# Attention masked by hashes with a maxout feed-forward layer: shorter zero products, a reshuffled first head, later bursts, halves of added weights added, own buffers for the last rows

## The chip, the core and the metric

The kernel runs on one core of one Trainium2 chip. A core has five engines that run at the same time, each with its own stream of instructions that it works through in order: TensorE (PE in the profile, with its weight loads as PEld), VectorE (DVE), ScalarE (ACT), GpSimd (POOL) and SyncE (SP), which here only issues DMAs. Engines wait for each other by semaphores. The metric is the device time of one execution in microseconds (us). The kernel before takes 277.81 us (median of 3 runs, 276.68 to 278.61).

## What is computed

The input is `q`, `k` and `v` for 4 batches of 8 heads with 768 positions of 64 numbers, a projection `proj` of 64 by 6, and the weights of a feed-forward layer (three matrices of 512 by 768 and `w_out` of 768 by 512). The core of the reference:

```
q_bits = (einsum('bhsd,dk->bhsk', q, proj) > 0)      # 6 sign bits per position
k_bits = (einsum('bhsd,dk->bhsk', k, proj) > 0)
mask   = bucket(q_bits)[..., :, None] == bucket(k_bits)[..., None, :]
scores = where(mask, q @ k^T / 8, -1e9)
attn   = softmax(scores)                             # over the keys
x      = (attn @ v), heads side by side              # 3072 rows of 512
h      = max(x @ w1, x @ w2, x @ w3)
out    = h @ w_out
```

The output is 3072 rows of 512 numbers in fp32.

## The kernel before, in words

**How the mask is made.** For each head the kernel keeps a tile `S` that holds, in bf16, the transposed and scaled 64 rows of q and k and below them rows with the sign bits as +0.5 and -0.5. One product of such columns gives the score plus a term that is largest where all bits agree; with the bias of the exponential, other keys fall to almost nothing.

**Chunks and units.** Queries are worked on in chunks: batch 0 has three chunks of 256 queries (chunks 0 to 2), batches 1 to 3 have two chunks of 384 each (chunks 3 to 8). A *unit* (`scores`, L277) is one chunk, one head and a part of the keys. For chunks 3 to 8 it is two score products of 384 columns (L293) and one exponential on ACT over 128 x 768 elements (L301), which writes a tile `AT` of unnormalized weights in fp16. There are 192 units; units 0 to 47 belong to batch 0, and each later chunk has 24. The 24 `AT` tiles are used in turn.

**Adding weights.** The softmax needs the sum of a query's weights over all keys. For chunks 3 to 8 the three `AT` tiles of a head (six blocks of 128 keys, two to a tile) are first added on DVE (`add`, L317 to L324): two additions of 128 x 768 per head, which leave a tile `ad` with two blocks of 384 columns. The additions of a unit are recorded two units later.

**Bursts.** When four heads of a chunk (a half chunk, 12 units in chunks 3 to 8) are through, `burst` (L333) runs three pieces: `sums` (L345) multiplies the blocks of `ad` by ones, 8 products for chunks 3 to 8, then a short chain on DVE turns the result into reciprocals (L352 to L356: transposition, addition, reciprocal, transposition back); `values`, twice, multiplies the weights by v (L367, 24 products each), and DVE scales the result into `xT` (L374). `LAG` sets how many units after its last unit a burst stands: 1 for chunks 0 to 2 (whose bursts have partly fixed places), 2 for the later ones (L557).

**Feed-forward.** A chunk's feed-forward layer is a list of groups (`ffn_groups`, L385): 18 groups of four products (L396), each followed by a copy (ACT, L401; DVE, L403, for chunks 0 to 2) or a maximum on DVE (L405), and then for each 128 rows two half groups of three products with `w_out` (L433), a copy to `osb` on ACT (L437) and a DMA to the output on SP's queue (L439). The pool of `osb` has two buffers. About one group (1.15 per unit after batch 0) is placed after the scores of a unit. The last 128 rows of the last chunk are made in two halves (`last`, L410): one is copied by ACT (L418) and sent from ACT's queue, the other by DVE (L420) and sent from SP's queue; each half takes an `osb` tile of its own.

**Banks.** The sums, values, hashes and feed-forward groups write to four PSUM banks handed out in turn (`bank`, `give`); scores have their own two. A product that gets a bank must wait until the engine that read its former content is through.

**Loads and transpositions.** Heads 0 to 7 of batch 0 are transposed on PE (`pair_turn`, L120), copied to fp32 tiles `T32` (`pair_keep`), hashed (`head_hash` L167 with `head_bits` L172, or `pair_hash`) and placed into `S` (`pair_place` on POOL, L134, or `first_place` on ACT, L161). For later batches, sets of four heads are transposed on DVE (`turn`, L198: eight transpositions of 128 x 384 for the q and k of a set), narrowed on POOL (L203), placed by DMAs on SP's queue (L208), and hashed by 16 products (`quad_hash`, L217) whose bits are made on DVE (L220) and placed by DMAs on SP's queue (L228). `hash_at` gives the unit of that hash: 11 units before the set is needed. v and the feed-forward weights are loaded by DMAs that POOL issues (L236, L244).

**Order.** The whole order is written out by hand inside `manual_schedule`: the loop at L572 records, unit by unit, the next scores, then the work due at this unit, then feed-forward groups, then bursts. Each engine works in this order; only the semaphores' waits decide the time. Before the loop stands the opening (L449 to L507): loads, clearing of tiles, 12 products of zeros (L472), and the first head's path to the first unit.

Of the kernel before, what the change touches and what calls it, by code (L numbers as in the profile page):

```python
# [9 lines left out]
FP32 = mybir.dt.float32  # L10
# [7 lines left out]
def kernel(  # L18
# [34 lines left out]
    NAT = 24  # L53
    LAG = 1
    ATW = 776
# [23 lines left out]
    at_tiles = [konst.tile([P, ATW], FP16, name=f"AT{i}", tag=f"AT{i}") for i in range(NAT)]  # L79
    warm = at_tiles[-1][:, 0:HALF]  # L80
    w_sb = [konst.tile([P, NJC, DF], FP16, name=f"w{i}_sb", tag=f"w{i}_sb") for i in range(3)]
# [6 lines left out]
    def bank():  # L88
        i = free_banks.pop(0)
        return i, bank_tiles[i]  # L90

    def give(i):
        free_banks.append(i)
# [69 lines left out]

    def head_hash(bp, pi, side, hd):
        for par in range(2):
            j = 2 * side + par
            nc.tensor.matmul(bp[Q * j : Q * j + NBITS, 0:HALF], pj2[:, par : 2 * NBITS : 2],  # L167
                             t32[pi][:, side, hd * HALF : (hd + 1) * HALF], start=True, stop=True)
# [105 lines left out]
    def block_of(b, m):  # L274
        return 2 * (m % MH) + m // MH if b == 0 else m
# [41 lines left out]
    def add(c, h, n):  # L317
        w = chunks[c][2]
        t = [blocks(at_tiles[at_of[unit_at[c, h, i]]], w)[:, :, 0:w] for i in range(n + 1)]
        if n == 1:  # L320
            sum_of[c, h] = ad_pool.tile([P, 2, HALF], FP16, tag="ad", name="ad")
        else:
            t[0] = sum_of[c, h][:]
        nc.vector.tensor_tensor(out=sum_of[c, h][:], in0=t[0], in1=t[n], op=AluOp.add)  # L324

    def sum_blocks(c, h):
        w = chunks[c][2]
        if (c, h) in sum_of:
            t = sum_of[c, h]
            return [t[:, j, 0:w] for j in range(2)]  # L330
        return [weights_of(c, h, m)[:, 0:w] for m in range(NM)]
# [53 lines left out]
    def ffn_groups(c):  # L385
# [22 lines left out]
        rows = out[b * S : (b + 1) * S, :].rearrange("(p c) m -> c p m", c=NM)  # L408

        def last(part, tb):  # L410
            k_, ps = bank()
            cs = slice(part * DM // 2, (part + 1) * DM // 2)
            for fb in range(NFB):
                nc.tensor.matmul(ps[:, 0 : DM // 2], hts[fb][:, tb * P : (tb + 1) * P], wout_sb[:, fb, cs],
                                 start=(fb == 0), stop=(fb == NFB - 1))
            osb = o_pool.tile([P, DM], FP32, tag="osb", name="osb")
            if part == 0:
# [6 lines left out]
        for tb in range(w // P):  # L424
            def go2(part, tb=tb):
# [9 lines left out]
                if part == 1:  # L435
                    osb = o_pool.tile([P, DM], FP32, tag="osb", name="osb")
                    nc.scalar.copy(osb[:], ps[:, 0:DM])  # L437
                    give(k_)
                    nc.sync.dma_start(rows[block_of(b, q0 // P + tb)], osb[:])  # L439
            gs += [lambda go2=go2: go2(0), lambda go2=go2: go2(1)]  # L440
# [7 lines left out]
    with tc.manual_schedule():  # L448
# [9 lines left out]
        load_pair(3, nc.sync)  # L458
        nc.gpsimd.memset(pj[:], 0.0)
        nc.vector.memset(pj2[:], 0.0)  # L460
# [3 lines left out]
        for hd in range(2):  # L464
            for u in range(2):
                nc.vector.tensor_copy(pj2[hd * D + u * Q : hd * D + (u + 1) * Q, hd : hd + 2 * NBITS - 1 : 2], pst[:, u, :])
        for x in range(4):
            nc.gpsimd.tensor_copy(pj[x * Q : (x + 1) * Q, :, x : x + 4 * NBITS - 3 : 4], pst[:])
        load_v(0)
        iw, wp = bank()  # L470
        for n in range(12):
            nc.tensor.matmul(wp[:, 0:HALF], warm[:, 0:P], warm, start=True, stop=True)  # L472
        give(iw)
# [3 lines left out]
        ib, bk = bank()  # L477
        i1, mk1 = bank()
        bq = sc_ps.tile([P, 2, 512], FP32, tag="sc", name="bp")[:, 0, :]
        pair_turn(0, 1, 0, mk)  # L480
        pair_turn(0, 0, 0, mq)
        pair_keep(0, 1, 0, mk)
        pair_keep(0, 0, 0, mq)
        head_hash(bk, 0, 1, 0)
        head_hash(bq, 0, 0, 0)
        pair_turn(0, 1, 1, mk1)
        first_place(1, 0, 0, mk)
        head_bits(bk, 0, 1, 0, 0)
        first_place(0, 0, 0, mq)
        head_bits(bq, 0, 0, 0, 0)  # L490
        give(iq)
        first_place(1, 0, 1, mk)
        head_bits(bk, 0, 1, 0, 1)
        give(ik)
        give(ib)
        pair_place(0, 0, 1, 0, 1)
        i2, mq1 = bank()
        pair_turn(0, 0, 1, mq1)
        pair_keep(0, 1, 1, mk1, nc.scalar)
        give(i1)  # L500
        scores(0)
        head_bits(bq, 0, 0, 0, 1)
        pair_keep(0, 0, 1, mq1, nc.scalar)
        give(i2)
        for side in (1, 0):
            for par in range(2):
                pair_place(0, side, par, 1, 2)  # L507

        for pi, us in ((1, ((0, 1, 0), (0, 0, 0), (3, 1, 1), (4, 0, 1))), (2, ((6, 1, 0), (7, 1, 1), (8, 0, 0), (9, 0, 1))),
# [26 lines left out]
        for g in range(2, NQUAD):  # L536
            b2, i2 = divmod(g, 2)
            need = UPB * b2 + 12 * i2
            for n, side in enumerate((1, 0)):
# [9 lines left out]
                when(t0 + 6, place, name, range(4))  # L549
            hash_at[{2: 33, 3: 47}.get(g, need - 11)] = g  # L550
            when({2: 36, 3: 46}.get(g, need - 22), load_v, g)
# [4 lines left out]
        for c, i in sorted(done_at, key=lambda e: done_at[e]):  # L556
            d = done_at[c, i] + (LAG if c < 3 else 2)  # L557
            sums, values = burst(c, i)
# [67 lines left out]
```

## Time and profile before

One execution was profiled. Its own time was 277.43 us, of which the span from its first to its last instruction is 275.6 us.

| | |
|---|---|
| median of 3 runs | 277.81 us |
| profiled execution: time, span | 277.43 us, 275.6 us |
| PE busy | 263.2 us (95%) |
| DVE busy | 196.0 us (71%) |
| ACT busy | 179.1 us (65%) |
| POOL busy | 68.0 us (25%) |
| sum products (L345) | 240 |
| additions of weights (L324) | 96, mean 551 to 572 ns |
| mean granted TensorE clock | 0.992 |

Busy time is time in which an engine executes; a matmul's end is modelled, so that the row of a product shows some 0.16 us more than the distance to the next one. The *view of waits* lists who waited for whom; the *chain* follows the work that ended last back from the end; the *table by stretches* gives busy times, the granted TensorE clock and DMA load between two times; the *timeline* lists instructions with the idle time of their engine before them and what ended it, in brackets.

### The profile page before, as it was taken

Reading aid. Unit: us, or ns where it says so; the run is one execution under the profiler, and the core shown is the slowest. Engines: PE = TensorE matmul, PEld = TensorE weight load, DVE = VectorE, ACT = ScalarE, POOL = GpSimd, SP = SyncE. Lnnn points to the kernel's source line nnn. Section 1 sums busy time; section 2 is a strip of 40 time slices with the busy share of each in tenths; the row PEclk is TensorE's granted clock in tenths of the full one; section 3 lists DMA queues with packets and bytes.
Section 4 is the critical chain, followed back from the end, with each engine's and each line's share of the span. In section 5 each row is a group of like instructions: output and inputs, shape, how many; then the busy total and the mean of one; then the engine's idle time right before and its main releaser. Section 6 shows DMA issues by size and latency. Waiting matters only on the chain.

```text
span 275.6 us, 6502 instructions
## 1 busy us (share of the span) xinstructions
PE 263.2 (95%) x2538; PEld 158.6 (58%) x2538; DVE 196.0 (71%) x486; ACT 179.1 (65%) x260; POOL 68.0 (25%) x108
## 2 busy tenths in 40 slices
PE   7899999999999979999999999999999999999992
PEld 3555667865666645565555555555555555555651
DVE  3686787965886996996684898797657674865440
ACT  2888876648767860966859586683868769571321
POOL 3699550374100350285000062140000000000000
PEclk9999999999999997999999999999999999999999
DMA  7979999979921157169912036622020003001203
GB/s 226 287 158 165 221 245 227 209 125 231 246 49 40 38 145 115 53 183 251 168 40 76 2 81 148 160 57 63 33 95 0 1 4 114 2 0 40 76 2 114
DMA packets 20398, 30.97 MB, mean 112 GB/s; under 512 B 2608, under 2 KB 14736, under 8 KB 20368
## 3 DMA queue, kind: packets, MB, share of 16 engines
q0 software_dynamic: 8384, 14.16, 26.9%
q1 hardware_dynamic: 11552, 15.88, 19.2%
q10 hardware_dynamic: 432, 0.52, 0.6%
q8 instruction: 20, 0.33, 0.5%
q14 instruction: 10, 0.08, 0.1%
HBM read 25.17 MB, written 6.29 MB: 114 GB/s over the span
## 4 chain that ended last, share of the span: by engine, by line
PE 86%; DVE 7%; ACT 2%; issue 2%; DMA 1%; DVEq 0%; ACTq 0%
PE ms L396 31%; PE sc L293 22%; PE ms L367 11%; PE ms L433 11%; PE ms L345 4%; PE ms L217 3%; ACT AT L301 2%; DVE ad L324 2%; PE ms L472 1%; DVE ht L405 1%; PE ms L120 1%; PE ms L147 1%; PE ms L167 1%; DVE S L172 1%; DMA out_dram<-osb 1%
## 5 line engine op out<-in xcount | busy, mean ns | idle before, releaser
L301 ACT ACTIVATE AT<-sc 128x768 f16<-128x768 f32 x192 | 152.7, 816 | 66.4 <-PE sc L293 58.6
L396 PE MATMUL ms<-xT,w_sb 128*128 128x384 f16 (+1 forms) x648 | 115.0, 308 | 0.7 <-DVE ht L405 0.7
L293 PE MATMUL sc<-S 72*128 72x384 bf16 (+1 forms) x432 | 93.5, 308 | 2.6 <-ACT AT L301 1.9
L396 PEld LDWEIGHTS <-w_sb 128*128 128x128 f16 x648 | 62.6, 97 | 36.9 <-issue 1.5
L405 DVE TENSOR_TENSOR ht<-ht,ms 128x384 f16<-128x384 f16 (+1 forms) x108 | 54.3, 503 | 37.3 <-PE ms L396 35.4
L293 PEld LDWEIGHTS <-S 72*128 72x128 bf16 (+1 forms) x432 | 39.5, 98 | 34.0 <-issue 14.1
L203 POOL TENSOR_SCALAR T<-T 128x768 bf16<-128x768 f32 x24 | 21.8, 907 | 101.2 <-DVE T L198 80.4
L367 PE MATMUL ms<-AT,vo 128*32 128x385 f16 (+3 forms) x864 | 37.7, 318 | 0.0
L433 PE MATMUL ms<-wout_sb,ht 128*128 128x512 f16 x138 | 35.4, 378 | 0.0
L367 PEld LDWEIGHTS <-vo 128*32 128x32 f16 x864 | 25.1, 99 | 9.3 <-issue 1.3
L324 DVE TENSOR_TENSOR ad<-AT,AT 128x768 f16<-128x768 f16 x48 | 27.4, 572 | 2.8 <-ACT AT L301 2.8
L324 DVE TENSOR_TENSOR ad<-ad,AT 128x768 f16<-128x768 f16 x48 | 26.5, 551 | 2.5 <-ACT AT L301 1.2
L198 DVE STREAM_TRANSPOSE T<-nat 128x384 f32<-128x384 f32 x48 | 26.6, 561 | 0.0
L401 ACT CAST ht<-ms 128x384 f16<-128x384 f32 x36 | 17.2, 477 | 8.8 <-PE ms L396 8.7
L374 DVE SCALAR_TENSOR_TENSOR xT<-ms,sv,rb 128x384 f16<-128x384 f32 (+1 forms) x36 | 19.9, 568 | 2.6 <-PE ms L367 1.3
L433 PEld LDWEIGHTS <-ht 128*128 128x128 f16 x138 | 13.3, 97 | 13.3 <-DVE ht L405 0.8
L437 ACT COPY osb<-ms 128x512 f32<-128x512 f32 x23 | 13.4, 582 | 10.7 <-PE ms L433 9.6
L352 DVE STREAM_TRANSPOSE ys<-ms 128x384 f32<-128x384 f32 (+1 forms) x18 | 9.7, 536 | 8.0 <-PE ms L345 7.8
L134 POOL TENSOR_SCALAR S<-T 64x384 bf16<-64x384 f32 (+1 forms) x21 | 13.2, 627 | 3.8 <-ACT T L127 1.6
L192 POOL DMA_DIRECT2D nat<-in_k_dram x20 | 11.1, 563 | 3.6 <-DMA nat<-in_k_dram 2.2
L192 POOL DMA_DIRECT2D nat<-in_q_dram x20 | 11.1, 566 | 2.7 <-DMA vo<-in_v_dram 1.8
L345 PEld LDWEIGHTS <-ones 128*32 128x32 f16 x240 | 5.4, 95 | 8.8 <-issue 8.7
(48 smaller groups left out, 121.9 us busy)
## 6 DMA issues: line engine op xcount, KB each, us to landing
out_dram<-osb SPq DMA_DIRECT2D x23, 256.0 KB
S<-T SPq DMA_DIRECT2D x48, 96.0 KB
nat<-in_k_dram POOLq DMA_DIRECT2D x20, 192.0 KB, 7.5
nat<-in_q_dram POOLq DMA_DIRECT2D x20, 192.0 KB, 7.1
vo<-in_v_dram POOLq DMA_DIRECT2D x8, 384.0 KB, 8.2
w_sb<-in_moe_w_dram POOLq DMA_DIRECT2D x3, 768.0 KB, 7.2
nat<-in_k_dram SPq DMA_DIRECT2D x6, 192.0 KB
nat<-in_k_dram SPq DMA_DIRECT2D x3, 384.0 KB
```

Of the source, the lines that this page charges most:

```text
L192: eng.dma_start(dst, src)
L198: nc.vector.transpose(t32[name][:, u, half * HALF : (half + 1) * HALF], i_)
L203: nc.gpsimd.tensor_scalar(out=t16[name][:, u, :], in0=t32[name][:, u, :], scalar1=RS, scalar2=1.0, op0=AluOp.mult, op1=AluOp.mult)
L293: nc.tensor.matmul(views[j], s_of[kn][0 : D + bits, kx, m * P : (m + 1) * P], s_of[qn][0 : D + bits, qx, q0 : q0 + w], start=True, stop=True)
L301: nc.scalar.activation(t[:, :, 0:w], whole, ActFn.Exp, bias=-SCALE * 0.25 * bits, scale=SCALE)
L324: nc.vector.tensor_tensor(out=sum_of[c, h][:], in0=t[0], in1=t[n], op=AluOp.add)
L367: nc.tensor.matmul(av[Q * x : Q * (x + 1), 0:n], v_at[2 * b + i][:, x, cb * D + side : (cb + 1) * D : 2], weights_of(c, 4 * i + x, m)[:, 0 ...
L374: nc.vector.scalar_tensor_tensor(out=xt_of(c)[:, 2 * i + side, 0:w], in0=av[:, 0:w], scalar=sv_of[b, i, side][:], in1=rb[0][:, 0:w], op0=A ...
L396: nc.tensor.matmul(ps[:, 0:w], w_sb[wi][:, jc, fb * P : (fb + 1) * P], xt[:, jc, 0:w], start=(jc == 0), stop=(jc == NJC - 1))
L401: nc.scalar.copy(hts[fb][:, 0:w], ps[:, 0:w])
L405: nc.vector.tensor_tensor(out=hts[fb][:, 0:w], in0=hts[fb][:, 0:w], in1=ps[:, 0:w], op=AluOp.max)
L433: nc.tensor.matmul(ps[:, 0:DM], hts[fb][:, tb * P : (tb + 1) * P], wout_sb[:, fb, :], start=(fb == 0), stop=(fb == NFB - 1))
```

## The change

- `warm`, the tile for the zero products, is 256 columns at another place of the last `AT` tile; 14 products of 256 columns replace 12 of 384. It is cleared in one instruction as before, of 256 instead of 384 columns.
- Opening: two of the four copies into the projection `pj2` go from DVE to POOL. Clearing and filling `pj` and the first load of v go from POOL's beginning to the end of the opening. The first head's k is kept by DVE and its q by ACT (both by DVE before); its placing is three times POOL and once ACT (before: three times ACT, once POOL); the hash products of k and q alternate; the first unit's scores stand before the second head's transpositions; the second head is kept by DVE instead of ACT.
- `LAG` becomes `(1, 4)`: bursts of chunks 3 to 8 stand four units behind instead of two.
- For chunks 4 to 8, after a head's second addition, DVE adds the second block of `ad` to the first (128 x 384), and `sums` reads one block: 4 products instead of 8.
- The last chunk's rows go to slices of one tile from the pool of loads, one slice per 128 rows, instead of the two `osb` buffers.
- The hash of a set stands 9 units ahead instead of 11.

```diff
-    LAG = 1
+    LAG = (1, 4)
-    warm = at_tiles[-1][:, 0:HALF]
+    warm = at_tiles[-1][:, THIRD + 2 : 2 * THIRD + 2]
...
         nc.vector.tensor_tensor(out=sum_of[c, h][:], in0=t[0], in1=t[n], op=AluOp.add)
+        if n == 2 and c > 3:
+            t = sum_of[c, h]
+            nc.vector.tensor_tensor(out=t[:, 0, :], in0=t[:, 0, :], in1=t[:, 1, :], op=AluOp.add)
...
-            return [t[:, j, 0:w] for j in range(2)]
+            return [t[:, j, 0:w] for j in range(1 if c > 3 else 2)]
...
+        def out_rows(tb):
+            if c < NCH - 1:
+                return o_pool.tile([P, DM], FP32, tag="osb", name="osb")
+            if "end" not in nat:
+                nat["end"] = nat_pool.tile([P, 4 * NM * D], FP32, tag="nat", name="nat")
+            return nat["end"][:, tb * DM : (tb + 1) * DM]
...
-        nc.gpsimd.memset(pj[:], 0.0)
...
             for u in range(2):
-                nc.vector.tensor_copy(pj2[hd * D + u * Q : hd * D + (u + 1) * Q, hd : hd + 2 * NBITS - 1 : 2], pst[:, u, :])
-        for x in range(4):
-            nc.gpsimd.tensor_copy(pj[x * Q : (x + 1) * Q, :, x : x + 4 * NBITS - 3 : 4], pst[:])
-        load_v(0)
+                (nc.vector, nc.gpsimd)[hd].tensor_copy(
+                    pj2[hd * D + u * Q : hd * D + (u + 1) * Q, hd : hd + 2 * NBITS - 1 : 2], pst[:, u, :])
         iw, wp = bank()
-        for n in range(12):
-            nc.tensor.matmul(wp[:, 0:HALF], warm[:, 0:P], warm, start=True, stop=True)
+        for n in range(14):
+            nc.tensor.matmul(wp[:, 0:THIRD], warm[:, 0:P], warm, start=True, stop=True)
...
         pair_keep(0, 1, 0, mk)
-        pair_keep(0, 0, 0, mq)
-        head_hash(bk, 0, 1, 0)
-        head_hash(bq, 0, 0, 0)
-        pair_turn(0, 1, 1, mk1)
-        first_place(1, 0, 0, mk)
+        pair_keep(0, 0, 0, mq, nc.scalar)
+        give(ik)
+        for par in range(2):
+            pair_place(0, 1, par, 0, 1)
+        first_place(0, 0, 0, mq)
+        give(iq)
+        pair_place(0, 0, 1, 0, 1)
+        for par in range(2):
+            head_hash(bk, 0, 1, 0, (par,))
+            head_hash(bq, 0, 0, 0, (par,))
         head_bits(bk, 0, 1, 0, 0)
-        first_place(0, 0, 0, mq)
         head_bits(bq, 0, 0, 0, 0)
+        scores(0)
+        i1, mk1 = bank()
+        pair_turn(0, 1, 1, mk1)
...
+        nc.gpsimd.memset(pj[:], 0.0)
+        for x in range(4):
+            nc.gpsimd.tensor_copy(pj[x * Q : (x + 1) * Q, :, x : x + 4 * NBITS - 3 : 4], pst[:])
+        load_v(0)
...
-            hash_at[{2: 33, 3: 47}.get(g, need - 11)] = g
+            hash_at[{2: 33, 3: 47}.get(g, need - 9)] = g
...
-            d = done_at[c, i] + (LAG if c < 3 else 2)
+            d = done_at[c, i] + LAG[c > 2]
```

## The prediction

> **What bounds the kernel now.** First the page's busy times: PE works 95% of the span, so a microsecond saved elsewhere counts only where PE stands still, at half clock, or has work removed.
>
> ```profile
> span 275.6 us, 6502 instructions
> PE 263.2 (95%) x2538; PEld 158.6 (58%) x2538; DVE 196.0 (71%) x486; ACT 179.1 (65%) x260; POOL 68.0 (25%) x108
> PEclk9999999999999997999999999999999999999999
> ```
>
> One slice of the clock is not full. The view of waits, for PE alone, shows where it stands:
>
> ```profile
> PE sc L293 <- ACT AT L301: 1.9, 4, 0.6
> PE ms L345 <- DVE ad L324: 1.8, 2, 1.4
> PE ms L472 <- DVE AT L463: 1.7, 1, 1.7
> ```
>
> Then the table by stretches (columns: length, then PE, PEld, DVE, ACT, POOL busy with instructions, clock, DMA share, GB/s). The first three rows lie between the sum products of one half chunk and the next: (3,0) to (3,1), on to (4,0), on to (4,1). The next two are the same for chunk 6, the last two are shorter.
>
> ```profile
> 74.11:87.85 13.74, 13.11 (x131) 8.38 (x130) 11.09 (x37) 9.58 (x14) 0.00 (x0) 1.00 0.26 64
> 87.85:103.96 16.11, 13.54 (x139) 9.16 (x139) 14.77 (x37) 10.51 (x14) 6.20 (x8) 1.00 0.33 96
> 103.96:121.44 17.48, 17.48 (x146) 10.31 (x145) 14.56 (x31) 10.64 (x16) 5.23 (x7) 0.90 0.46 105
> 154.27:169.17 14.90, 14.90 (x129) 8.29 (x128) 14.30 (x32) 10.71 (x16) 6.12 (x8) 1.00 0.28 76
> 169.17:186.31 17.14, 17.14 (x153) 9.88 (x152) 14.53 (x31) 11.79 (x19) 3.98 (x5) 1.00 0.50 115
> ...
> 100.62:104.03 3.41, 1.54 (x17) 0.92 (x18) 3.31 (x9) 1.00 (x2) 1.85 (x2) 1.00 0.30 69
> 104.04:107.46 3.42, 3.42 (x48) 2.09 (x51) 2.38 (x6) 0.00 (x0) 0.00 (x0) 0.50 1.05 143
> ```
>
> In the half chunks in which DVE also transposes a set, it is nearly full. In 87.85 to 103.96 it is the bound; the timeline shows the sum products waiting for its additions:
>
> ```profile
> 103.36 0.55 DVE L324 TENSOR_TENSOR ad<-ad,AT 128x768 f16<-128x768 f16 x1
> 103.83 0.41 DVE L403 CAST ht<-ms 128x256 f16<-128x256 f32 x1
> 103.96 0.75 PE L345 MATMUL ms<-ad,ones 128*32 128x384 f16 x5 [1.45 <-DVE ad L324]
> ```
>
> After 3.41 us with PE busy for 1.54, the clock is 0.50 for 3.42 us: 1.7 us lost.
>
> **Opening: taken as 0.** The zero products start at 1.67, behind DVE's clearing of the last weights tile, and the changed program still waits for that clearing. They stand 0.32 us apart; twelve would end at 5.51, yet the first transposition starts at 5.27, so the rate doubles near 5.05. Fourteen of 256 columns at 2/3 of 0.32 end at 1.67 + 3.0 = 4.6: transpositions start 0.67 earlier, the first 1.6 at half rate (0.27), the rest at 0.137 (six in 0.82). But the first bits decide:
>
> ```profile
> 6.87 0.82 PE L167 MATMUL bp<-T,pj 128*6 128x384 f32 x4
> 7.27 0.56 DVE L172 TENSOR_SCALAR S<-ms 6x384 bf16<-6x384 f32 x1 [0.46 <-PE ms L167]
> 8.46 0.49 PE L293 MATMUL sc<-S 70*128 70x256 bf16 x3
> ```
>
> In the changed program the first bits wait for the third hash product (k, second half), behind one of q that needs ACT's copy of q. They end at 4.6 + 0.45 + 0.6 = 5.65, ACT's copy (0.48) ends at 6.30, the third product starts at 6.63, bits at 7.26: as before. Bounds: 0.9 earlier if the third product isn't waited for, 0.6 later if the transpositions stay slow. The six transpositions now between units 0 and 1 (0.82) fill the 0.69 us in which PE waited there. POOL gets two placings more (0.5 each) and, behind the second head's placing, the clearing, four copies and load of v that stood ahead (1.1 + 0.94), so that its queue to 33 us runs 3 us late: loads of k, w1, q and w2 are behind it. Its placings for head 2 would end at 16.7 against a use at 20.07; the q set would land near 36 against a first transposition at 35.26, which DVE makes up by 41, where it idles 1.05 us. No cost; if that cover is gone, up to 1 us.
>
> **Half chunks of chunk 4: -1.5 us.** PE's own work from rows: two score products 0.325, a feed-forward group 0.65 (0.44 for 256 columns), sums 0.33, values 1.95, a hash 1.3. The second row holds 12 units, 13 narrow groups, 3 products of 0.216 and a burst: 12.5 of 16.1, so 3.6 lost; the third 15.5 of 17.5, so 2.0 lost, the clock's 1.7 among them. Together 5.6.
>
> No row shows the addition of 128 x 384 within SBUF. Two additions of twice the size start 0.47 apart when independent (246.32 and 246.79) and 0.66 when the second needs the first (246.79 and 247.45). Half of 0.47 plus the 0.19 of dependence is 0.42, which I take; ends 0.22 (the wait hidden) and 0.66 (size without effect). Four to a half chunk are 1.7 us of DVE. Against that a burst two units later gives DVE room: behind the last halving that it needs there now stand a copy, two maxima, a transposition and an addition, 0.31 + 2 x 0.33 + 0.49 + 0.44 = 1.9. Second row after: 14.77 + 1.7 - 1.9, plus 0.56 from the sum products to DVE's first step and 0.4 idle, is 15.5 against 11.8 of PE (fewer groups fall here): 3.7 lost. Third: 14.56 + 1.7 = 16.2 against 15.8: 0.4. Together 4.1: the wait moves from the sum products to feed-forward groups that need a bank. Spread over five places at 0.5 to 1.0 it leaves PE busy for 1.9 or more of any 3.41 us; the trace keeps the clock at 2.71 and drops it at 1.54, so I take it as kept. Bounds: 5.6 gained, 0.5 lost.
>
> **Sums: -1.6.** 40 products fewer, four side by side: 0.33 to 0.163 for each of ten bursts.
>
> **Chunk 6: +0.3.** First half: 14.30 + 1.7 - 1.9 + 1.0 = 15.1 of DVE against 15.1 of PE. Second: 14.53 + 1.7, less what the later burst moves out, 16.1 against 15.8. Without sets (chunks 5, 7, 8; 10 of 17 us busy from 186.31) DVE has room. Bounds 0 and 3. The hash, moved with its burst, sends its bits (DMAs on SP behind output rows that ACT has copied) some 7 units ahead of use, 3 us to spare: nothing.
>
> **Last burst: +0.85.** It can't move back: the units are over. Its sum products waited 0.37 for the last addition (ended 248.01); two halvings now stand in that chain, 0.84.
>
> **Last rows: -1.55.** The timeline of the end:
>
> ```profile
> 269.26 1.47 PE L414 MATMUL ms<-wout_sb,ht 128*128 128x256 f16 x12
> ...
> 270.94 0.37 ACT L418 COPY osb<-ms 128x256 f32<-128x256 f32 x1 [0.84 <-DMA out_dram<-osb]
> 271.34 0.35 ACTq L422 DMA_DIRECT2D out_dram<-osb  x1
> 272.30 0.42 DVE L420 COPY osb<-ms 128x256 f32<-128x256 f32 x1 [4.79 <-DMA out_dram<-osb]
> ```
>
> Both copies wait for a DMA to leave an `osb` buffer, though PE is done at 270.73. With own slices DVE's copy starts at 270.75. Next late is the transfer itself; the three last writes now overlap, at worst 0.5 worse.
>
> **Sum:** 0 - 1.5 - 1.6 + 0.3 + 0.85 - 1.55 = -3.5, from the profiled execution's 277.43 to 273.9. That execution lies 0.4 below the median, so I say **274.0**.
>
> **Rivals.**
> 1. *The later bursts free PE wholly.* For it: two units are 2 us, about the 1.9 that DVE gains. Against: DVE's work in the second row exceeds PE's by 3. Another 3.7 and 0.9 in the opening: 269.4. Chance 0.17.
> 2. *The clock still falls.* For it: PE loses as much time as before in that half chunk. Against: it is spread. Its 1.7 stays: 275.7. Chance 0.20. The Trainium skill ("TensorE: Matmul & The Clock Gate", on HAM oscillation) wants idle gaps above some 3.4 us for a drop; the longest here is 1.45 us, so by it this drop has another cause and stays. The trace speaks against that: the drop comes right behind the emptiest 3.41 us.
> 3. *Slower: the halvings fill DVE.* A halving at 0.66 costs 0.24 more in the eight of chunk 4, the six or so of chunk 6 that PE would feel, and the last two: 3.8; with a second drop of the clock and chunk 6 at its bound, 277.43 - 3.5 + 3.8 + 1.7 + 1.7 = 281. It decides from about 0.67 alone, 0.55 with one drop. Chance 0.10.
> 4. *The opening doesn't bring the first unit forward*: that is in my forecast; the first exponential stays near 8.98.
>
> The forecast has 0.53. A measurement tells about 1% of this kernel. Its spread of 1 us lies mostly below 275.0: faster 0.60, same 0.28, slower 0.12. Range 270.5 to 277.2: it holds the second rival and the near end of the first.
>
> **What would show it.** First exponential at 8.9 to 9.0; 200 sum products; 40 halvings at some 0.3 to 0.4 us each; waits of PE for DVE's maxima of 2 to 4 us between 95 and 108, none for DVE's additions before the last burst; clock 1.0 throughout; the last DVE copy 0.05 us behind PE. Wrong would make me: PE at 100% around 100 us, a clock of 0.50 anywhere, or waits for maxima in chunk 6.

## The result, and the profile after

The changed kernel takes **290.42 us** (median of 4 runs, 289.67 to 292.42) beside 277.88 of the kernel before. The ratio is 1.0467, with a 95% interval of 1.0403 to 1.0531. Slower by 4.7%, where 1.4% faster was forecast. The profiled execution took 290.16 us, with a span of 288.4.

The page of the changed kernel, with the lines that answer to those of before and two of the chain that ended last:

```profile
span 288.4 us, 6456 instructions
PE 264.9 (92%) x2500; PEld 156.8 (54%) x2500; DVE 212.2 (74%) x525; ACT 178.2 (62%) x257; POOL 69.8 (24%) x112
PEclk9999995999999999999979999999999999999999
...
PE 68%; DVE 12%; DMA 9%; issue 3%; POOL 3%; ACT 2%; SPq 1%; DVEq 0%; ACTq 0%; POOLq 0%
PE ms L399 24%; PE sc L293 16%; PE ms L443 10%; PE ms L370 9%; DMA vo<-in_v_dram 4%; DMA S<-bits 3%; PE ms L217 3%; DVE ad L324 3%; DVE ht L408 2%; ACT AT L301 2%; DVE T L198 2%; PE ms L348 2%; POOL S L134 2%; DMA S<-T 2%; DVE ad L327 1%
```

PE has less to do (38 instructions fewer) and its share falls from 95% to 92%. The clock has two holes, in the seventh and the twenty-first slice; the hole of before, at 104 us, is gone. The chain holds two transfers that the prediction priced at nothing: a load of v and the bits of a set.

The view of waits of the changed kernel, for PE alone (columns: us in total, times, longest):

```profile
PE ms L370 <- DMA vo<-in_v_dram: 3.7, 1, 3.7
PE sc L293 <- DMA S<-bits: 3.5, 1, 3.5
PE ms L399 <- DVE ht L408: 2.7, 5, 0.7
PE ms L443 <- DVE ht L408: 2.5, 3, 1.3
PE sc L293 <- ACT AT L301: 1.8, 4, 0.6
PE ms L348 <- DVE ad L327: 1.7, 2, 1.2
```

The first two are single waits, the next two are spread over the half chunks in which DVE transposes a set. The table by stretches (columns: length, then PE, PEld, DVE, ACT, POOL busy with instructions, clock, DMA share, GB/s) shows both. The first three rows run from the sum products of one half chunk to the next, (3,0) to (4,1); the next two are those of chunk 6; the last five lie at the two waits:

```profile
82.63:96.87 14.24, 13.71 (x134) 8.66 (x134) 10.60 (x34) 10.52 (x16) 0.00 (x0) 1.00 0.16 43
96.87:113.87 17.00, 13.37 (x136) 8.81 (x136) 16.48 (x40) 10.02 (x13) 6.41 (x8) 1.00 0.35 82
113.87:131.55 17.68, 16.35 (x141) 9.18 (x140) 16.99 (x36) 10.83 (x16) 6.78 (x10) 1.00 0.49 117
168.99:185.90 16.91, 15.71 (x127) 8.29 (x126) 15.67 (x34) 11.59 (x18) 6.42 (x8) 1.00 0.39 86
185.90:202.68 16.78, 16.23 (x146) 9.09 (x146) 15.62 (x33) 11.56 (x18) 3.90 (x4) 1.00 0.43 108
...
40.42:43.83 3.41, 0.75 (x24) 0.46 (x23) 3.20 (x12) 1.20 (x2) 2.01 (x3) 1.00 1.19 259
43.83:47.24 3.41, 2.33 (x44) 1.72 (x48) 1.05 (x3) 0.00 (x0) 0.99 (x2) 0.50 1.08 242
47.24:50.66 3.42, 3.42 (x31) 0.88 (x19) 0.64 (x2) 0.81 (x1) 0.00 (x0) 0.50 1.16 256
142.82:146.23 3.41, 0.12 (x1) 0.00 (x0) 1.57 (x4) 0.38 (x1) 0.00 (x0) 1.00 0.74 131
146.23:149.65 3.42, 3.25 (x11) 1.56 (x12) 0.00 (x0) 1.73 (x3) 0.00 (x0) 0.50 0.00 1
```

DVE fills 16.48 of 17.00 and 16.99 of 17.68 us in chunk 4, and PE stands for 3.63 and 1.33. At 41 and at 143 us PE is nearly empty for 3.4 us, and the clock is 0.50 behind it, for 6.83 and 3.42 us. At 41 us the DMA engines are full all the time; at 143 us their share is 0.74 and falling, behind 1.21 in the 3.42 us before. (The share adds up the times of all packets, so that it can exceed 1.)

**Where the 12.7 us of span went** (275.65 before, 288.38 after). The starts of the exponentials of equal units in both traces give the order of events. That of the first unit starts 0.37 us later than before. That of unit 32, before the wait for v, is 0.2 later; of unit 49, behind it, 7.0. Unit 102, behind the last burst of chunk 4, is 8.1 later, unit 114, behind the wait for the bits, 12.8. Unit 150, behind chunk 6, is 14.4 later, unit 186 13.6, and the end 12.7. So v and the clock behind it cost 6.8, the bits and the clock behind them 4.7, chunks 4 and 6 some 2.7; 0.8 comes back between units 150 and 186, and the end gives 0.9 back.

The last rows did what was forecast, as the timeline of the changed kernel shows:

```profile
283.52 1.47 PE L424 MATMUL ms<-wout_sb,ht 128*128 128x256 f16 x12
...
284.37 0.37 ACT L428 COPY nat<-ms 128x256 f32<-128x256 f32 x1
...
285.03 0.42 DVE L430 COPY nat<-ms 128x256 f32<-128x256 f32 x1 [3.27 <-PE ms L424]
```

PE ends at 284.99, DVE's copy starts at 285.03 and has waited for PE, no longer for an output write. The time lies elsewhere.

### The profile page after: what moved, and what is told of

Its sections match the earlier page's. It is cut to its first block, busy times and chain, and to the rows that moved or that the text cites. A ratio compares the mean times of both kernels' runs of the same rounds, so it can differ in the third digit from the quotient of the medians.

```text
span 288.4 us, 6456 instructions
## 1 busy us (share of the span) xinstructions
PE 264.9 (92%) x2500; PEld 156.8 (54%) x2500; DVE 212.2 (74%) x525; ACT 178.2 (62%) x257; POOL 69.8 (24%) x112
## 4 chain that ended last, share of the span: by engine, by line
PE 68%; DVE 12%; DMA 9%; issue 3%; POOL 3%; ACT 2%; SPq 1%; DVEq 0%; ACTq 0%; POOLq 0%
PE ms L399 24%; PE sc L293 16%; PE ms L443 10%; PE ms L370 9%; DMA vo<-in_v_dram 4%; DMA S<-bits 3%; PE ms L217 3%; DVE ad L324 3%; DVE ht L408 2%; ACT AT L301 2%; DVE T L198 2%; PE ms L348 2%; POOL S L134 2%; DMA S<-T 2%; DVE ad L327 1%
## 5 line engine op out<-in xcount | busy, mean ns | idle before, releaser
L399 PE MATMUL ms<-xT,w_sb 128*128 128x384 f16 (+1 forms) x648 | 116.2, 310 | 3.7 <-DVE ht L408 2.7
L293 PE MATMUL sc<-S 72*128 72x384 bf16 (+1 forms) x432 | 94.5, 311 | 6.7 <-DMA S<-bits 3.5
L203 POOL TENSOR_SCALAR T<-T 128x768 bf16<-128x768 f32 x24 | 22.2, 926 | 112.8 <-DVE T L198 93.7
L370 PE MATMUL ms<-AT,vo 128*32 128x385 f16 (+3 forms) x864 | 36.6, 317 | 3.9 <-DMA vo<-in_v_dram 3.7
L370 PEld LDWEIGHTS <-vo 128*32 128x32 f16 x864 | 23.5, 99 | 15.9 <-issue 4.3
L324 DVE TENSOR_TENSOR ad<-AT,AT 128x768 f16<-128x768 f16 x48 | 26.7, 556 | 0.4 <-ACT AT L301 0.4
L327 DVE TENSOR_TENSOR ad<-ad 128x384 f16<-128x384 f16 x40 | 18.4, 459 | 1.4
L447 ACT COPY osb<-ms 128x512 f32<-128x512 f32 x21 | 12.2, 582 | 10.5 <-PE ms L443 7.2
L134 POOL TENSOR_SCALAR S<-T 64x384 bf16<-64x384 f32 (+1 forms) x23 | 14.2, 618 | 5.8 <-DVE T L129 4.3
L406 DVE CAST ht<-ms 128x256 f16<-128x256 f32 x18 | 7.4, 413 | 6.2 <-PE ms L399 6.0
```

The lines of the kernel that those rows point to most:

```text
L134: nc.gpsimd.tensor_scalar(out=o, in0=i_, scalar1=RS, scalar2=1.0, op0=AluOp.mult, op1=AluOp.mult)
L203: nc.gpsimd.tensor_scalar(out=t16[name][:, u, :], in0=t32[name][:, u, :], scalar1=RS, scalar2=1.0, op0=AluOp.mult, op1=AluOp.mult)
L293: nc.tensor.matmul(views[j], s_of[kn][0 : D + bits, kx, m * P : (m + 1) * P], s_of[qn][0 : D + bits, qx, q0 : q0 + w], start=True, stop=True)
L327: nc.vector.tensor_tensor(out=t[:, 0, :], in0=t[:, 0, :], in1=t[:, 1, :], op=AluOp.add)
L370: nc.tensor.matmul(av[Q * x : Q * (x + 1), 0:n], v_at[2 * b + i][:, x, cb * D + side : (cb + 1) * D : 2], weights_of(c, 4 * i + x, m)[:, 0 ...
L399: nc.tensor.matmul(ps[:, 0:w], w_sb[wi][:, jc, fb * P : (fb + 1) * P], xt[:, jc, 0:w], start=(jc == 0), stop=(jc == NJC - 1))
```

## The experiments

Two theories stood at the start. By the first, the two single waits are two separate causes, each a DMA that the change issues too late; each can be undone alone, and what is left is the price of the halvings. By the rival, DVE, which now adds 40 times more, is late everywhere, and the two waits only show where PE happened to stand.

### The hash at 11 again

```diff
-            hash_at[{2: 33, 3: 47}.get(g, need - 9)] = g
+            hash_at[{2: 33, 3: 47}.get(g, need - 11)] = g
```

> The changed kernel with the hash of a set 11 units ahead again, all else changed. Theory: the bits of the set for unit 108 leave two units (about 2 us) later, behind the loads of the next sets on the DMA engines, and land only at 146.4; PE waits 3.45 us and then works 3.41 us at half clock. With the hash back both go: 290.4 - 3.45 - 1.7 = 285.2 us, no wait of PE for the bits. Rival: the bits are late because the DMA engines are full whenever the later bursts let the loads start, so two units of lead don't help: 289 us or more, with a wait for the bits left.

Measured: 285.91 us (285.06 to 286.77), ratio 1.0281 [1.0233, 1.0328]. 4.5 us less than the changed kernel, and no wait for bits is left. The wait for v stays:

```profile
PE ms L370 <- DMA vo<-in_v_dram: 4.2, 1, 4.2
```

### POOL's beginning as before

Clearing and filling `pj` and the first load of v stand ahead of the opening again; everything else is as changed.

```diff
+        nc.gpsimd.memset(pj[:], 0.0)
+        for x in range(4):
+            nc.gpsimd.tensor_copy(pj[x * Q : (x + 1) * Q, :, x : x + 4 * NBITS - 3 : 4], pst[:])
+        load_v(0)
         iw, wp = bank()
...
-        nc.gpsimd.memset(pj[:], 0.0)
-        for x in range(4):
-            nc.gpsimd.tensor_copy(pj[x * Q : (x + 1) * Q, :, x : x + 4 * NBITS - 3 : 4], pst[:])
-        load_v(0)
```

> The changed kernel with the clearing and filling of pj and the first load of v at POOL's beginning again. Theory: the second load of v, issued at 32.46 instead of 29.01, lands at 44.87 instead of 35.58; PE waits 3.74 us and works two stretches of 3.41 us at half clock. With POOL's order back that goes: 290.4 - 3.7 - 3.4 = 283.3 us, load landed before 40. Rival: it is the two placings more on POOL and the full DMA engines that make it late, not the moved load: half of the wait or more stays, 286 us or more.

Measured: 284.35 us (281.44 to 285.29), ratio 1.0190 [1.0115, 1.0264], 6 us less than the changed kernel. The second load of v (issued by POOL at L236, used by the products with v at 41 us) is issued at 30.51 us and landed at 40.53, instead of 32.46 and 44.87, and PE no longer waits for it. The bits' wait is now the first in the list of PE's waits:

```profile
PE sc L293 <- DMA S<-bits: 3.1, 2, 2.9
```

### Both undone

The two edits above together.

> Both of these undone: hash 11 units ahead, POOL's beginning as before. Theory: the two losses are independent, 290.4 - 5.2 - 7.1 = 278.1 us, the clock at 1.0 throughout. Rival: one loss hides the other, or a third wait comes up behind them: 281 us or more.

Measured: 280.65 us (279.32 to 284.04, 10 runs), ratio 1.0092 [1.0061, 1.0123]. Together they give back 9.8 of the 12.5 us, about the sum of the two alone (4.5 and 6.1). So they are two causes, and they don't stand for one another: the first theory holds for this part. What is left, 0.9% over the kernel before, is more than the 278.1 that the theory had and close to the 281 of the rival, which allowed for a third wait behind them; the halvings, below, are one. The profiled execution was the slowest of the ten (284.04) and shows a wait for v of 2.9 us; the other nine lie between 279.32 and 282.59, four of them with a mean clock of 0.992 to 0.994 and five with 0.999 or 1.0. It seems that this load is on the edge even with POOL's beginning as before; only one of the ten was traced.

### Are nine units too few, or are the DMA engines full?

In the changed kernel the bits of the set for unit 108 are issued on SP's queue from 136.30 to 139.24 us, and PE has them at 146.40. The DMAs that fill the engines meanwhile are POOL's loads of the next set (`load_quad`, at `need - 36`): POOL runs ahead of the units. The DMA view of the changed kernel from the last bits' issue to PE's start (139.24 to 146.40; columns: packets, MB, share of 16 engines) shows POOL's queue, q0, beside the one that SP uses, q1:

```profile
q0 software_dynamic: 784, 1.15, 88.2%
q1 hardware_dynamic: 160, 0.10, 7.6%
```

The next kernel leaves the hash at 9, has POOL's beginning as before, and issues those loads from SP, where they stand behind the bits:

```diff
-                        when(need - 36 + 4 * n + x, load_quad, side, g, (x,), nc.gpsimd)
+                        when(need - 36 + 4 * n + x, load_quad, side, g, (x,), nc.sync)
```

> The changed kernel with POOL's beginning as before (284.35 us), in which the hash 9 units ahead still costs a wait of PE for S<-bits (2.92 us) and a clock of 0.50 behind it. Here the loads of the natural rows of sets 4 and up are issued from SP's queue, behind the bits' DMAs, instead of from POOL's, which runs ahead of the units; the hash stays at 9. Theory: the bits are late because POOL's set loads fill the DMA engines (over 90% in the stretch behind their issue); with those behind them they land within 3.5 us of their issue, PE doesn't wait for them and the clock stays: 280.7 us, between 279.5 and 282. Rival: nine units are too few even with free DMA engines, since DVE's products of the hash end too late: PE waits 2 us or more for S<-bits again, 283.5 or more.

Measured: 279.13 us (278.15 to 280.16, 10 runs), ratio 1.0053 [1.0024, 1.0081]; a little below the expected range, and 5.2 us less than with POOL's loads. The timeline of SP's queue in this kernel:

```profile
130.22 2.94 SPq L228 DMA_DIRECT2D S<-bits  x4
133.20 1.39 SPq L192 DMA_DIRECT2D nat<-in_k_dram  x3
```

The bits are issued at the same time as with POOL's loads (130.37 to 133.31 there), with the same nine units, and nobody waits for them; in this trace the clock stays at 1.0. The packets of the bits (160 on q1) show the difference. With POOL's loads the first one starts at 135.29 and the last one ends at 139.42, 6.1 us behind the last issue; here they are through at 133.99, 0.8 us behind it. So nine units are enough with free DMA engines. What made them too few is the company: in the changed kernel four DMAs of 24 KB beside loads of 192 KB took some 7 us from the last issue to PE's start.

The kernel before had little to spare either: the last packet of these bits ends at 133.95, and PE uses them at 134.78. In the run with own last rows alone, described below, whose hash stands at 11, the timeline of PE shows a wait for the same bits:

```profile
135.15 0.48 PE L293 MATMUL sc<-S 72*128 72x384 bf16 x2 [0.45 <-DMA S<-bits]
```

### What makes v late

Three kernels, all with the hash at 11 (285.91 us), take POOL's moved work apart. The first moves only the load of v back to the beginning, the second only the clearing and copies of `pj`; the third keeps POOL's opening as changed and records the second load of v ahead of four loads of q:

```diff
-        when(17, load_v, 1)
...
+        when(13, load_v, 1)
         when(13, load_quad, 0, 2, range(4), nc.gpsimd)
```

> The changed kernel with the hash at 11 (285.91 us; PE waits 4.20 us for the second load of v, and a clock of 0.50 follows), and of POOL's moved work only the first load of v back at the beginning; the clearing and four copies of pj stay behind the placings. Theory Q: the second load of v is late because it is issued later into DMA engines that SP's loads of the next set have filled, whatever stands ahead of it in POOL's queue; issued about 1 us earlier it lands some 3 us earlier, PE waits 1 to 2.5 us, no or one window of 0.50: 282 to 284. Rival T: the traffic of the first load (384 KB), moved behind the opening, is what holds the second up; with it away the wait is gone: 280.7, as with all of POOL's beginning put back.

> The same with only the clearing and the copies of pj back at the beginning, and the first load of v behind the placings. Theory Q: about 1 us of POOL's queue again, the second load of v lands some 3 us earlier: 282 to 284, like the run with the load alone. Rival T: nothing gained, 285.5 or more.

> The changed kernel with the hash at 11 (285.91 us) and POOL's beginning as the change has it; only the second load of v is issued at unit 13, ahead of POOL's four loads of q, instead of at unit 17. Theory Q: it gets the DMA engines before SP's loads of the next set do, lands some 8 us earlier, and PE's wait and the clock's drop go: 280.7, between 279.5 and 282, though the q set lands later (DVE's transpositions then wait, which DVE can make up). Rival: the DMA engines are the bound in this stretch and the wait only moves to q's set: 283.5 or more.

The times and ratios are of all executions, the other columns of the one that was traced:

| | time, us | ratio | second v issued | landed | PE waits | clock 0.50 for |
|---|---|---|---|---|---|---|
| as changed, hash 11 | 285.91 | 1.0281 [1.0233, 1.0328] | 32.84 | 45.68 | 4.20 | 3.41 |
| load alone early | 283.84 | 1.0215 [1.0175, 1.0255] | 31.57 | 43.96 | 2.35 | 3.41 |
| `pj` alone early | 281.03 | 1.0131 [1.0089, 1.0173] | 31.57 | 42.73 | 1.39 | none |
| second v ahead of q | 285.66 | 1.0300 [1.0259, 1.0342] | 25.86 | 37.37 | none for v | 6.83 |

The traffic of the first load is not the cause: with the load late and `pj` early, nearly all is given back. Both halves bring the issue to 31.57, 1.3 us sooner, and the landing 1.7 and 2.95 us sooner. That the two runs differ by 2.8 us, more than theory Q allowed, goes with the clock: a wait of 2.35 us still costs a stretch at 0.50, one of 1.39 doesn't.

The third run went against theory Q's main sentence. v lands eight us sooner and nothing is gained. The view of waits of that kernel, for PE and for DVE:

```profile
PE ms L348 <- DVE xT L377: 4.1, 1, 4.1
...
DVE T L198 <- DMA nat<-in_q_dram: 7.1, 1, 7.1
```

q's set, now behind v, landed at 42.61 instead of 38.24; DVE waits 7.1 us at its first transposition, the scaling into `xT` stands behind that in DVE's queue, and PE waits for the bank that `xT` frees. The rival is right: in this stretch the DMA engines are the bound. Their share is 0.94 or more in every 4 us from 28 to 48 us of all four kernels, and in the kernel before too (1.05, 1.25, 1.08, 1.10, 1.22); what is issued there lands later by more than it is issued later (v: issued 3.45 us later, landed 9.29 later), and the order only picks who waits.

### What the halvings cost

Both stalls undone, and no halvings: sums of two blocks as before, bursts still four units behind.

```diff
-        if n == 2 and c > 3:
+        if n == 2 and c > 99:
...
-            return [t[:, j, 0:w] for j in range(1 if c > 3 else 2)]
+            return [t[:, j, 0:w] for j in range(2)]
```

(No chunk has a number above 99, so that nothing is halved.)

> Both undone, and no halvings: the sum products read two blocks again, bursts stay four units behind. Theory: DVE's 40 more additions (18.4 us busy) cost more than the 1.6 us of products that they save: the waits for DVE in chunk 4 (4.9 us) shrink to about 2, those of chunk 6 (1.9) and 0.8 at the last burst go, 278.1 - 2.9 - 1.9 - 0.8 + 1.6 = 274 us. Rival: DVE had the room, and the products come back as a loss: 279.7 us.

Measured: 275.53 us, the median of four executions, of which one took 1501.24 us; the other three took 274.17, 274.27 and 276.79. The ratio without the long one is 0.9891 [0.9824, 0.9958]: faster than the kernel before. The halvings with their shorter sums cost 5.1 us by these medians, 5.6 by the ratios, and 6.2 by the medians without the longest execution of either kernel; the theory had some 4 (278.1 less 274) and the rival next to nothing. Where, the gaps of PE in the two traces tell: chunk 4 has 5.1 us with them and 1.75 without; chunk 6 has 2.4 and none; the wait ahead of the last burst's sums is 1.15 and 0.37. That is 6.5 us of waits, less some 1.6 of shorter sums. (The trace with halvings is of that kernel's longest execution; the one with `pj` alone early, without a drop of the clock, has the same gaps in chunks 4 and 6.)

The timeline of the changed kernel shows that the halvings are of two kinds (some lines left out):

```profile
101.53 0.98 POOL L203 TENSOR_SCALAR T<-T 128x768 bf16<-128x768 f32 x1 [24.00 <-DVE T L198]
...
101.85 0.86 DVE L327 TENSOR_TENSOR ad<-ad 128x384 f16<-128x384 f16 x1
...
106.05 0.36 DVE L327 TENSOR_TENSOR ad<-ad 128x384 f16<-128x384 f16 x1
...
110.04 1.05 POOL L203 TENSOR_SCALAR T<-T 128x768 bf16<-128x768 f32 x1 [1.83 <-DVE T L198]
...
110.43 0.86 DVE L327 TENSOR_TENSOR ad<-ad 128x384 f16<-128x384 f16 x1
```

Of the sixteen halvings in the four rows of chunks 4 and 6, eight start while POOL narrows a set (L203) and take 0.86 to 0.87 us; the other eight, and the 24 outside these rows, take 0.36. So the halvings are dearest where DVE is fullest. No run moves a halving away from POOL's narrowing, so that its part of the 5 us stays open.

The next kernel keeps the halvings but takes both blocks to the sums, so that PE saves nothing:

```diff
-            nc.vector.tensor_tensor(out=t[:, 0, :], in0=t[:, 0, :], in1=t[:, 1, :], op=AluOp.add)
+            nc.vector.tensor_tensor(out=t[:, 1, :], in0=t[:, 0, :], in1=t[:, 1, :], op=AluOp.add)
...
-            return [t[:, j, 0:w] for j in range(1 if c > 3 else 2)]
+            return [t[:, j, 0:w] for j in range(2)]
```

> The kernel with both stalls undone (POOL's beginning and the hash 11 units ahead: 280.65 us), and the halvings kept, each now written into the second block, while the sum products take both blocks again (20 products and 0.33 us a burst instead of 10 and 0.163). The denominators then count the first block twice, so this run prices PE's part alone. Theory: the shorter sums are worth their 1.6 us, since each stands in PE's own queue: 282.2. Rival: where DVE sets the end (chunks 4 and 6) PE waits anyway, and only the bursts of chunks 5, 7 and 8 pay: 281.2 or less. Halvings cost what is left between this run and the one without them (275.5): 6.7 by the theory, 5.7 or less by the rival.

Measured: 281.53 us (280.63 to 282.32), ratio 1.0123 [1.0079, 1.0168], 0.9 over the kernel with short sums. The intervals of the two ratios overlap, so that neither 1.6 nor 0.5 is excluded; the value lies nearer to the rival's. The rows from one half chunk's sums to the next tell more. In the two traces the six rows in which PE has no gap are 0.16 to 0.17 us longer with long sums, 1.0 together; the two that start at the last burst of chunk 5 and at the first of chunk 6 differ by -0.01 and 0.13, since PE waits for DVE in them. In chunk 4 PE's gaps are 4.5 instead of 5.1 us; the traced execution, the longest of the four, has a drop of the clock there that the other kernel doesn't have, so that these rows can't be compared in length. So a shorter sum pays where PE is the bound, and hardly where it waits.

### Last rows and later bursts on the kernel before

First the last rows alone (`out_rows` of the change, on the kernel before), then the four units of delay with them:

```diff
-            d = done_at[c, i] + (LAG if c < 3 else 2)
+            d = done_at[c, i] + (LAG if c < 3 else 4)
```

> The kernel before with the last rows in buffers of their own and nothing else of the change. Theory: DVE's last copy no longer waits for an output write to leave its buffer and starts within 0.1 us of PE's last product; 1.55 us less than before: 276.7 beside a 278.24 of before. Rival: the three last writes, now overlapping, land later and eat the gain: 277.7 or more.

> The kernel before with the last rows in buffers of their own and the bursts of chunk 3 on four units behind; opening, hash at 11 and two sum blocks as before. Theory: the two units free PE of most waits in the second half chunks of chunk 4 (5.6 us lost before, 1.75 in the kernel without halvings) and of the clock's drop: 276.7 - 3 = 273.7, or 274.5 if the drop was no whole loss. It then beats the kernel with the change's opening and without halvings (275.5), and the opening is worth less than nothing. Rival: before's opening costs what the change's one gains, or the later bursts bring only 1 us: 275.5 or more.

Measured: 276.42 us (12 runs, ratio 0.9947 [0.9918, 0.9976]) beside 277.90, which is 1.5 less, as the theory had it. With the delay 273.41 us (272.71 to 273.53), ratio **0.9827 [0.9791, 0.9863]**: another 3.0, in the theory's place too. The table by stretches of the second kernel, cut at its own sum products, with the columns of the table above, shows (3,0) to (4,1) and chunk 6:

```profile
76.21:90.45 14.24, 13.71 (x134) 8.67 (x134) 10.59 (x34) 10.65 (x16) 0.00 (x0) 1.00 0.16 45
90.45:106.12 15.67, 14.24 (x149) 9.01 (x148) 15.29 (x39) 9.43 (x13) 6.21 (x8) 1.00 0.35 89
106.12:122.98 16.86, 16.61 (x150) 8.97 (x150) 15.01 (x32) 11.39 (x17) 8.73 (x13) 1.00 0.63 150
154.07:171.22 17.15, 17.15 (x148) 8.74 (x148) 14.41 (x31) 11.65 (x18) 6.21 (x8) 1.00 0.47 102
171.22:187.64 16.42, 16.42 (x149) 9.04 (x148) 14.29 (x30) 11.39 (x18) 3.91 (x4) 1.00 0.39 106
```

Without halvings PE is full in chunk 6, stands for 1.43 and 0.25 us in chunk 4, and the clock is 1.0. DVE has 15.29 and 15.01 us of work there; in the changed kernel 16.48 and 16.99, in rows that are longer by 1.3 and 0.8.

This kernel beats the one with the change's opening and without halvings by 0.9 us (274.27, the median without the execution of 1501.24), or, by the ratios, by 0.6%; their intervals overlap. That the change's opening gains anything isn't shown; whether it costs something stays open.

### Halvings where DVE is idle

The same, with the halvings in chunks 5 and 7 alone:

```diff
+        if n == 2 and c in HALVED:
+            t = sum_of[c, h]
+            nc.vector.tensor_tensor(out=t[:, 0, :], in0=t[:, 0, :], in1=t[:, 1, :], op=AluOp.add)
...
-            return [t[:, j, 0:w] for j in range(2)]
+            return [t[:, j, 0:w] for j in range(1 if c in HALVED else 2)]
```

> The kernel before with the last rows in own buffers, the bursts four units behind (273.41 us so far), and the halvings in chunks 5 and 7 alone, where DVE is idle 10 of 17 us. Theory: the four shorter bursts are worth 0.163 us each and nothing waits for the halvings: 272.8. Rival: halvings cost wherever they stand, since the maxima that feed-forward groups wait for queue behind them: 273.4 to 275.

Measured: 272.84 us (272.27 to 274.66), ratio 0.9844 [0.9808, 0.9879], beside a kernel before that was itself lower here (277.23). By the medians 0.6 less than without, by the ratios 0.2% more: no difference that can be told by the times. In the traces the stretch from the sums of (3,0) to those of (8,1) takes 168.23 us, against 168.71 without halvings; three of the four bursts pay 0.16 to 0.17 each. All 16 halvings take 0.36 us, none beside POOL's narrowing. So halvings don't cost their price where DVE is idle; that they gain half a microsecond there is seen in one trace of each kernel and not in the times.

## Why the prediction was wrong, point by point

**The step that failed first: "No cost; if that cover is gone, up to 1 us."** The opening's step saw that POOL's queue runs 3 us late and named what stands behind it as "loads of k, w1, q and w2". The second load of v stands there too and was not named. It is the one that PE waits for. The wait for q's set, which the step did follow, came as well: it landed at 38.37 instead of "near 36", and DVE waited 3.06 us for it. The step also took a delay of issue for a delay of landing. The DMA share in the trace of before was above 1 from 28 us on; three rows of it would have been a warning that 3 us of issue need not be 3 us of landing. Cost 6.8 us, against bounds of 0 and 1.

**The second: "the hash ... 3 us to spare: nothing."** The step doesn't say what it allowed for the landing. In the changed trace the bits are issued from 136.30 to 139.24 and PE stops for want of them at 142.95, 6.65 us behind the first issue, where the step had some 7 units; 3 us to spare leave under 4 us for issue and landing. They took 10.0: the last packet ends at 146.11 and PE is released at 146.26. In the kernel before, the bits are issued from 125.94 to 128.88 and used at 134.78; in a run with 11 units PE already waits 0.45 us. The two units were the slack. Cost 4.7 us, against bounds that had no such term.

**Chunk 4: "5.6 before" and "4.1 after".** The loss before was worked out as the length of the rows less PE's work from the prices of single rows. The table that stood on the same page gives it directly: 16.11 less 13.54, 2.57 us, none in the third row, and the clock's 1.7, together 4.3. After the change it is 3.63 and 1.33, 4.96. So instead of a gain of 1.5 there was a loss of 0.7. Of the 2.2 between them, 1.3 is the side before and 0.9 the side after. On that side two terms were mis-sized. The rows were to be 15.5 and 16.2 long and are 17.0 and 17.7, with DVE busy for 16.48 and 16.99. In each the four halvings keep DVE busy for 2.44 and 2.45 us instead of the 1.7 that was taken for them. In the first of the two rows the rest of DVE's work is 14.04 us, 0.7 less than the 14.77 of before, where the relief by the later burst was to be 1.9; in the second no relief was assumed, and the rest is 14.54 beside 14.56. With the later bursts alone DVE has no less to do in these rows than before (15.29 and 15.01 us); what the delay takes away is PE's wait for the additions and the clock's drop. Alone it is worth 3.0 us.

**The halving's price: "0.42, which I take".** Right for 32 of the 40. Near the end of the trace a halving starts 0.59 us behind the addition that it needs and the next instruction 0.28 behind the halving, where two additions alone stand 0.47 apart: 0.40, with 0.36 of them busy. The eight beside POOL's narrowing cost 0.87 by the same reckoning, more than the 0.66 that was set as the upper end, and they stand in the rows that had no room. That makes 8 x 0.45 = 3.6 us of DVE time that the forecast did not have. So the mechanism of rival 3, "the halvings fill DVE", which had a chance of 0.10, is what the runs show for this part: its own sum for dearer halvings was 3.8, and with both stalls gone the kernel takes 280.65 beside its 281. How near the two times lie is luck in part: the 281 holds a second drop of the clock, and the trace with `pj` alone early (281.03) has none.

**Chunk 6: "+0.3", bounds 0 and 3.** 1.75 us of PE's gaps in the changed kernel (1.20 and 0.55), none before. Inside the bounds; the four halvings of each row again keep DVE busy for 2.4 us instead of 1.7. Waits for maxima in chunk 6 were named as a sign of being wrong, and they are what these gaps are.

**Sums: "-1.6".** 0.9 measured, with an interval that holds 1.6. By the traces six bursts pay their 0.163 in full; three of the others stand at rows in which PE waits for DVE, where a shorter sum mostly makes the wait longer.

**Last burst "+0.85", last rows "-1.55".** Right: the wait ahead of the last burst's sums grew from 0.37 to 1.15, by 0.78; own rows gave 1.5 alone.

**The opening: "taken as 0".** The first exponential starts at 9.35 instead of 8.98. The transpositions start at 4.60, as reckoned, but all six stand 0.21 us apart: in this trace the clock goes up at 6.28, where the step had put it at 5.05, the place of the trace before. In the four traces whose opening is that of before it goes up between 4.66 and 7.02, so that 5.05 was the place of one execution and no price to build on. The step's bound of "0.6 later if the transpositions stay slow" covers the 0.37.

**The clock.** "Spread over five places ... I take it as kept": right for chunk 4 of the changed kernel, whose windows of 3.41 us hold 2.10 and 2.51 us of PE work at the least, with no drop. It was near: with halvings and long sums the window of 1.71 us, shown below, was followed by a drop. Rival 2, which kept the loss of 1.7 there, was wrong in its place; the clock fell elsewhere, at waits that the prediction had not seen.

**The sum.** Taken together from the changed trace, with PE's work, its idle time and the clock as the parts: opening 0.2 (by unit 32), v 6.8, bits 4.7, rows of chunks 4 and 6 at 6.7 of PE's idle time instead of 2.6 and the clock's 1.7, 2.4; last burst 0.8, sums -1.6 (as work) and last rows -1.5. That is 11.8 of the 12.7. The forecast's own last step is off by 0.3: 273.9 and the 0.4 by which the traced execution lies below the median make 274.3.

## What to carry to other kernels

Before an issue is moved later, list every DMA behind it on that queue, and read the DMA share in the stretch where they land: at a share near 1 a microsecond of issue can cost three of landing, and reordering only picks another victim. Read slack from landing to use, not from issue to use. Work that takes time from one engine and gives it to another is worth what the table by stretches says row by row: halvings that cost nothing where DVE is idle cost PE 5.8 us of waits in four rows where DVE had been busy for 0.83 to 0.96 of the time. And take the price of an instruction from the rows in which it will stand, beside what the other engines do there: a halving cost 0.40 us in one place and 0.87 in another.

## What the runs showed of the hardware

**The clock goes by half-empty windows of 3.41 us on a grid.** Between the opening and the end, all stretches at 0.50 in these traces are 3.41 or 6.83 us long. Cutting each trace into windows of that length, aligned to its own change of clock, gives PE's busy time in the window ahead of each drop: 0.00, 0.12, 0.56, 0.75, 0.87, 1.06, 1.15, 1.54, 1.71 and 1.71 us. The lowest ones behind which the clock stayed have 1.74, 1.76, 1.87, 1.87 and 1.90. In the kernel with halvings and long sums (length, PE busy, clock, DMA share, GB/s):

```profile
102.65:106.06 3.41, 1.71 (x13) 1.00 0.27 72
106.06:109.47 3.41, 3.31 (x18) 0.50 0.78 91
```

In the changed kernel with the hash at 11:

```profile
120.06:123.47 3.41, 1.74 (x10) 1.00 0.02 5
123.47:126.88 3.41, 3.41 (x22) 1.00 0.59 169
```

So here a window with PE busy for about half of its 3.41 us or less is followed by a window at 0.50, whatever the length of the single gaps: the longest gap at the first was 1.32 us, while the second, behind which the clock stayed, has one of 1.67. The Trainium skill ("TensorE: Matmul & The Clock Gate", Part 1) describes a gate that watches free-running windows of 3413 ns; the traces agree with that length. The same page of the Trainium skill, on HAM oscillation, asks for idle gaps above some 3.4 us; the traces have drops behind gaps of 1.32 and 1.45 us, so here the share of the window tells and the single gap doesn't. How much work a window at 0.50 needs to end the throttling isn't clear: 2.66 us ended it once, 3.04 in another run didn't.

**A small DMA waits for large ones of another queue.** Four DMAs of 24 KB, issued from SP, were there 6.1 us after the last issue while POOL's loads filled the engines, and 0.8 us after it when those loads stood behind them on SP's queue. This is read from the packets of the two kernels with nine units and POOL's beginning as before; with POOL's loads none of the bits' packets started in the first 4.9 us after the first issue.

**A halving on DVE takes longer beside POOL's narrowing.** In the nine traces with halvings in chunks 4 to 8, all 72 halvings that start while POOL narrows a set (128 x 768, fp32 to bf16, about 1 us) take 0.86 to 0.87 us and end 0.2 us behind the narrowing; the 288 others take 0.36. In all 14 traces the additions of 128 x 768 that start beside a narrowing take 0.67 to 0.69 us at the median instead of 0.55, while the transpositions (0.56 and 0.57) and maxima are no longer than elsewhere. What holds the additions up isn't shown by any run.
